# Rank-20 last products from the third token tile on, and plain ones for the second

## The chip, the cores and the metric

The kernel runs on one core of one Trainium2 chip. The metric is device time in microseconds of one execution: median 750.37 over three runs of the kernel before (750.37, 750.37, 753.23). The engines are named as in the profile: PE is the matrix engine (PEld its weight loads), DVE is VectorE, ACT is ScalarE, POOL is GpSimd, SP is the engine that issues most transfers.

## The reference

```python
def _attn_ref(q, k, v):                       # (8, 8, 576, 64) each
    scores = scale * np.matmul(q, k.transpose(0, 1, 3, 2))
    ...
    Dmat = np.where(rel >= 0, gamma[:, None, None] ** rel[None, :, :], 0.0)
    return np.matmul(scores * Dmat[None, :, :, :], v)

def _moe_ref(x, w1, w2, w3, w_out):           # x: (4608, 512), w: (512, 768), w_out: (768, 512)
    h = np.maximum(np.maximum(x @ w1, x @ w2), x @ w3)
    return (h @ w_out).astype(np.float32)
```

A retention block (attention with a decay instead of a softmax) makes x, 4608 tokens of 512 values. A feed-forward block takes the maximum of three products with x, called h (768 values a token), and multiplies it by w_out. All matrices are fp32 (the four weights come as fp64 words and are converted on the chip).

## The kernel before

The 4608 tokens are cut into 9 tiles t = 0 to 8 of 512 tokens. A tile has three stages of work, interleaved on PE: the attention of the next tile, in small matmuls; the three products with w1, w2, w3, called up; and the last product with w_out, called downs. Tile 0 runs while the weights are still converted, and takes its products plainly (`up_plain`, `downs_plain`).

For later tiles `up` (L756 for its matmuls) forms the three products by a scheme with 20 products in place of 24, in five chains A to E; it writes h in three groups fp of 256 hidden values, in the order 0, 2, 1. A product is two matmuls of 128x256. ACT copies chain values to tiles called `part` (L741), and DVE joins them by additions and maxima into h (L744).

`downs` takes the last product by a scheme of seven products in place of eight. Tokens, outputs and hidden values are each split in two; `sums_of_hidden` (L517) forms four sums of h for each group (two on DVE, two on POOL), and `sums_of_outs` forms, once, in tile 1, sums of w_out called To. Each of the seven products has six matmuls of 128x256, two for each group, that add up in one PSUM bank: dx, dy, dz, with two pools of banks, `ps_x` and `ps_y`, of two banks each. The order is written out by hand: 1 in dx, 2 in dy, 6 in dx, 7 in dz, 5 in dx, 4 in dz, 3 in dx. After a product ACT copies its bank to a `part` (`kept`, L560, or L605 for an output), or DVE adds a `part` to it (`total`, L570) and SP stores the result, 256 KB at a time. In the last tile dx is three pieces in banks of their own, so that the last copy and store are small.

Other work is put between the matmuls by hand. `soon` appends steps of VectorE and loads to a queue `urgent`; `chore(n)` emits n of them, or of a second queue, `chores`; `scale(n)` emits n of ACT's scalings of v by head (L191). Each `yield` of `ffn` lets the main loop emit the next entry of `steps(t)`: loads, transposes, scores (L310), values (the o matmuls, L427 and L434) of the next tile. In `downs` the yields stand after the products 2 and 4, and `values` of the next tile's last chunks come at the first of them.

Waits between engines are put in by the framework, from the tiles that instructions read and write; each engine then runs its queue in order.

Of the kernel before, what the change touches and what calls it, by code (L numbers as in the profile page):

```python
# [48 lines left out]
C = 128  # L49
# [25 lines left out]
         "A7": [("A1", ("A1", "B6"), ALU.add), ("A1", ("A1", "A5"), ALU.max), ("A1", ("A1", "A7"), ALU.max)]}  # L75
X_SUMS, W_SUMS = ([x.split() for x in text.split(",")] for text in (X_SUMS, W_SUMS))
PRODUCTS = [x.split() for x in PRODUCTS.split(",")]
# [4 lines left out]
def kernel(  # L82
# [33 lines left out]
    opool = ctx.enter_context(tc.tile_pool(name="opool", bufs=2))  # L116
# [32 lines left out]
    low = const.tile([P, P], FP32, name="low")  # L149
    for c in range(2):  # L150
        r = slice(D * c, D * (c + 1))
        nc.gpsimd.tensor_copy(low[r, 0:D], causal[r, r])
# [150 lines left out]
    def chunk_scores(g):  # L303
# [12 lines left out]
        def mask():  # L316
            nc.vector.tensor_tensor(st[:], s[:], low[:, 0:D].unsqueeze(1).to_broadcast([P, H, D]), op=ALU.mult)
# [137 lines left out]
    def sums_of_x(t, i):  # L455
        if i == CPT - 1 and t > 0:
            xS[t] = {f"a{r + 1}{d + 1}": xT[t][:, d, NH * r:NH * (r + 1)] for r in range(2) for d in range(NDC)}
            xS[t].update(late["X"])
            made[t] = {n for n in xS[t] if n[0] == "a"}

            def step(n, dst, _, a, sign, b):
                combine(*(xS[t][x] for x in (dst, a, b)), sign)
                if dst not in (later[0] for later in X_SUMS[n + 1:]):
                    made[t].add(dst)

            for n, line in enumerate(X_SUMS):
                soon(partial(step, n, *line))
# [36 lines left out]
    def sums_of_outs():  # L504

        pool = late["pool"]
        lo, hi = slice(0, DM // 2), slice(DM // 2, DM)
        b11, b12, b21, b22 = (w_out[:, :, e, r] for e in range(2) for r in (lo, hi))
        t1, t2, t4 = (pool.tile([P, NF // 2, DM // 2], FP32, name=f"To{n}")[:] for n in (1, 2, 4))

        sums = ((t1, b12, b11), (t2, b22, t1)), ((b12, b22, b12), (t4, b21, t2))
        late["sums of T"] = [partial(nc.vector.tensor_tensor, *(x[:, fp] for x in step), op=ALU.subtract)
                             for steps in sums for step in steps for fp in (0, 2, 1)]
        late["T"] = {1: b11, 2: b21, 3: b22, 4: t4, 5: t1, 6: t2, 7: b12}
        late["S"] = {n: pool.tile([P, NF // 2, NH], FP32, name=f"H{n}") for n in (1, 2, 3, 4)}

    def sums_of_hidden(h, fp):  # L517
        s1, s2, s3, s4 = (late["S"][n][:, fp, :] for n in (1, 2, 3, 4))
        a11, a12, a21, a22 = (h[:, 2 * fp + e, NH * r:NH * (r + 1)] for r in range(2) for e in range(2))
        vec, pool = nc.vector.tensor_tensor, nc.gpsimd.tensor_tensor  # L520
        urgent.append(lambda: vec(s1, a21, a22, op=ALU.add))
        urgent.append(lambda: vec(s2, s1, a11, op=ALU.subtract))
        urgent.append(lambda: (pool(s3, a11, a21, op=ALU.subtract), pool(s4, a12, s2, op=ALU.subtract)))  # L523

    def downs(t, h, order):

        def raw_hidden(r, e):
            return lambda fp: h[:, 2 * fp + e, NH * r:NH * (r + 1)]

        def summed(n):  # L530
            return lambda fp: late["S"][n][:, fp, :]

        NM = NH // P
        whole = slice(None)
        last = t == N // NT - 1
        hS = {1: raw_hidden(0, 0), 2: raw_hidden(0, 1), 3: summed(4), 4: raw_hidden(1, 1),
              5: summed(1), 6: summed(2), 7: summed(3)}

        banks = {}

        def bank(pool, tag, name):
            b = pool.tile([P, NM, DM // 2], FP32, tag=tag, name=name)
            pieces = [(m, whole, b[:, m, :]) for m in range(NM)]
            banks[id(pieces)] = [(whole, whole, b[:])]
            return pieces

        def together(src):
            return banks.get(id(src), src)

        def product(n, out, first):  # L550
            for fp in order:
                for m, cols, o in out:
                    nc.tensor.matmul(o, lhsT=hS[n](fp)[:, m * P:(m + 1) * P], rhs=late["T"][n][:, fp, cols],  # L553
                                     start=first and fp == order[0] and (m == 0 or last and out is x),
                                     stop=fp == order[-1], skip_group_check=True)

        def kept(src):
            both = ppool.tile([P, NM, NH], FP32, tag="part", name="part")
            for m, cols, o in together(src):
                nc.scalar.copy(both[:, m, cols], o)  # L560
            return both

        def store(r, c, osb, blocks=slice(None), cols=whole, queue=nc.sync):
            block = out[t * NT + r * NH:t * NT + (r + 1) * NH, c * (DM // 2):(c + 1) * (DM // 2)]
            queue.dma_start(block.rearrange("(m p) d -> p m d", p=P)[:, blocks, cols], osb[:, blocks, cols])

        def total(r, c, src, others):
            osb = opool.tile([P, NM, DM // 2], FP32, tag="osb", name="osb")
            for m, cols, o in together(src):
                nc.vector.tensor_tensor(osb[:, m, cols], o, others[:, m, cols], op=ALU.add)  # L570
            store(r, c, osb)

        if last:
            pieces_of_x = [(0, whole, ps_x), (1, slice(0, DM // 4), ps_r), (1, slice(DM // 4, DM // 2), ps_r)]
            x = []
            for m, cols, pool in pieces_of_x:
                b = pool.tile([P, NH], FP32, tag="x" if pool is ps_x else "r", name="dx")
                x.append((m, cols, b[:, :len(range(NH)[cols])]))
        else:
            x = bank(ps_x, "x", "dx")  # L580
        product(1, x, True)
        p1 = kept(x)
        yield
        y = bank(ps_y, "y", "dy")
        product(2, y, True)
        total(0, 0, y, p1)
        yield
        product(6, x, False)
        u2 = kept(x)
        yield  # L590
        z = bank(ps_y, "y", "dz")
        product(7, z, True)
        p7 = kept(z)
        yield
        product(5, x, False)
        total(1, 1, x, p7)
        yield
        product(4, z, False)
        total(1, 0, z, u2)
        yield  # L600
        osb = opool.tile([P, NM, DM // 2], FP32, tag="osb", name="osb")
        for group in ([[piece] for piece in x] if last else [x]):
            product(3, group, False)
            for m, cols, o in together(group):
                nc.scalar.copy(osb[:, m, cols], o)  # L605
            queue = nc.scalar if last and group[0] is x[-1] else nc.sync
            store(0, 1, osb, slice(group[0][0], group[-1][0] + 1), group[0][1], queue)
        yield
# [109 lines left out]
    def late_room():  # L718
        pool = late["pool"]
        late["W"] = [pool.tile([P, NF, P], FP32, name=f"n{n}") for n in range(1, 9)]  # L720
        late["X"] = {n: pool.tile([P, NH], FP32, name=n)[:] for n in sorted({x[0] for x in X_SUMS})}
# [40 lines left out]
    def downs_plain(t, h):  # L762

        ps = [(ps_x, ps_y)[m % 2].tile([P, DM], FP32, tag="xy"[m % 2], name="down") for m in range(NT // P)]
        for fb in range(NF):
            for m, b in enumerate(ps):
                nc.tensor.matmul(b[:], lhsT=h[:, fb, m * P:(m + 1) * P], rhs=w_sb["out", fb],  # L767
                                 start=(fb == 0), stop=(fb == NF - 1))
                if fb == NF - 1:
                    osb = opool.tile([P, DM], FP32, tag="osb", name="osb")  # L770
                    nc.scalar.copy(osb[:], b[:])
                    nc.sync.dma_start(out[t * NT + m * P:t * NT + (m + 1) * P, :], osb[:])
# [39 lines left out]
    def ffn(t):  # L812

        h = hpool.tile([P, NF, NT], FP32, tag="h", name="h")
        if t == 0:
# [19 lines left out]
            for fb, _ in enumerate(downs_plain(t, h)):  # L835
                convert(2 if fb < 2 else 4 * len(pieces))
                if fb == 2:
                    while_converting.close()
                    late["pool"] = ctx.enter_context(tc.tile_pool(name="late", bufs=1))
                    state_factors()  # L840
                    late_room()
                    sums_of_outs()
# [8 lines left out]
        if t == 1:  # L851
            spread.append(True)
            weight_sums(2)
            weight_sums(1)
        total = len(order) * 2 * len(PRODUCTS)
        count = parts = 0
        for fp in order:
# [13 lines left out]
            sums_of_hidden(h, fp)  # L871
        chore(len(urgent))
        for n, _ in enumerate(downs(t, h, order)):
            if t == 1 and n in (0, 2):
                for step in late["sums of T"][3 * n:3 * n + 6]:
                    step()  # L876
            chore(4)
            scale(2)
            if n in (1, 3):
                yield  # L880
# [148 lines left out]
```

## Time and profile before

| | |
|---|---|
| runs | 750.37, 750.37, 753.23 us |
| profiled execution | 749.71 us, of which the span is 748.0 |
| granted clock of PE | 1.00 |
| busy, of the span | PE 99%, PEld 82%, DVE 69%, ACT 44%, POOL 9% |
| one tile's window (338 to 417 us) | PE 79.0 of 79 us, DVE 52.1, ACT 35.1, POOL 7.8 |

In the groups of the profile a row has the line, the engine, the operation, output and inputs, the shape, the count, then total busy time and the mean of one in ns, and the idle time of the engine just before them with its releaser. In the timeline a row has the start, the length, the engine, the line, the operation and the count; a group of a matmul's records is merged to one row, and the ends of matmuls are modelled. In the chain of waits a row has start, length, engine, tile and count.

### The profile page before, as it was taken

To read this page: it belongs to the slowest core of one execution; us is meant where nothing else is said; L and a number is where in the kernel's file an instruction comes from. 1 tells how busy PE (TensorE), PEld (TensorE's weight loads), DVE (VectorE), ACT (ScalarE), POOL (GpSimd) and SP (SyncE) were. 2 spreads that over 40 slices of the span, in tenths; PEclk is the share of its full clock that TensorE was granted. 3 is DMA by queue.
4 is the path that set the end of the run, shared out by engine and by line. 5 is a ranking of instruction groups with operands and counts; after the bars stand their busy time and mean duration, and the time that the engine had idled before them with its cause. 6 is when DMAs were issued, how large, how long until landed. Compare 5 with 4: busy or idle time off the path is not lost.

```text
span 748.0 us, 16662 instructions
## 1 busy us (share of the span) xinstructions
PE 742.1 (99%) x6768; PEld 615.2 (82%) x6768; DVE 518.5 (69%) x884; ACT 327.1 (44%) x657; POOL 69.3 (9%) x85
## 2 busy tenths in 40 slices
PE   8999999999999999999999999999999999999998
PEld 7645547888888888888888888888888888888887
DVE  3998989998766765686667756774767656763662
ACT  4664533454245424543354435543554255414441
POOL 3000000022000100010010101010101010100000
PEclk9999999999999999999999999999999999999999
DMA  9996742515242514241434224232514141000001
GB/s 224 237 254 140 210 92 74 97 18 96 64 81 46 99 38 95 42 84 44 96 62 73 57 67 90 47 78 61 100 27 88 55 88 31 2 29 29 1 0 57
DMA packets 230205, 59.31 MB, mean 79 GB/s; under 512 B 210800, under 2 KB 228848, under 8 KB 230128
## 3 DMA queue, kind: packets, MB, share of 16 engines
q1 hardware_dynamic: 228720, 57.91, 35.5%
q8 instruction: 53, 0.87, 0.5%
q10 hardware_dynamic: 1408, 0.33, 0.2%
q14 instruction: 24, 0.20, 0.1%
HBM read 48.76 MB, written 9.44 MB: 78 GB/s over the span
## 4 chain that ended last, share of the span: by engine, by line
PE 97%; DVE 1%; DMA 1%; issue 0%; ACT 0%; POOL 0%; POOLq 0%; DVEq 0%
PE a L756 19%; PE b L756 17%; PE dx L553 11%; PE c L756 9%; PE up L780 8%; PE d L756 6%; PE dz L553 6%; PE e L756 6%; PE sk L310 3%; PE down L767 3%; PE dy L553 2%; PE o L427 2%; PE o L434 2%; PE s L288 1%; DMA qraw<-in_q_dram 1%; PE o L396 1%
## 5 line engine op out<-in xcount | busy, mean ns | idle before, releaser
L744 DVE TENSOR_TENSOR part<-part 128x512 f32<-128x512 f32 x168 | 116.0, 691 | 104.8 <-ACT part L741 102.3
L741 ACT COPY part<-b 128x512 f32<-128x512 f32 x120 | 70.2, 585 | 150.6 <-PE b L756 150.5
L744 DVE TENSOR_TENSOR h<-h,part 128x512 f32<-128x512 f32 x120 | 83.7, 697 | 28.1 <-ACT h L741 24.0
L741 ACT COPY part<-a 128x512 f32<-128x512 f32 x96 | 56.2, 585 | 49.9 <-PE a L756 49.2
L756 PE MATMUL a<-s,w 128*128 128x256 f32 x288 | 73.9, 379 | 0.0
L756 PE MATMUL b<-s,n 128*128 128x256 f32 x288 | 73.9, 379 | 0.0
L191 ACT ACTIVATE vraw<-vraw,gk 128x64 f32<-128x64 f32 x208 | 65.4, 346 | 2.2 <-DMA vraw<-in_v_dram 2.1
L780 PE MATMUL up<-xT,w 128*128 128x512 f32 (+2 forms) x160 | 64.0, 554 | 0.0
L756 PEld LDWEIGHTS b<-s,n 128*128 128x128 f32 x288 | 54.7, 190 | 7.4
L756 PEld LDWEIGHTS a<-s,w 128*128 128x128 f32 x288 | 54.7, 190 | 7.4
L780 PEld LDWEIGHTS up<-xT,w 128*128 128x128 f32 x160 | 28.6, 190 | 29.9 <-issue 26.5
L327 POOL TENSOR_TENSOR s<-s,gs_of 64x512 f32<-64x512 f32 x21 | 22.3, 1062 | 320.6 <-DVE s L325 191.2
L756 PE MATMUL c<-xT,w 128*128 128x256 f32 x192 | 51.3, 389 | 0.0
L756 PE MATMUL d<-s,w 128*128 128x256 f32 x192 | 49.8, 380 | 0.0
L756 PE MATMUL b<-xT,n 128*128 128x256 f32 x192 | 49.3, 379 | 0.0
L523 POOL TENSOR_TENSOR H<-h 128x256 f32<-128x256 f32 x24 | 20.2, 843 | 305.3 <-DVE h L744 305.3
L553 PE MATMUL dx<-To,H 128*128 128x256 f32 (+1 forms) x204 | 44.8, 370 | 0.5 <-DVE To L876 0.5
L756 PE MATMUL e<-xT,w 128*128 128x256 f32 x192 | 45.4, 379 | 0.0
L756 PE MATMUL a<-xT,n 128*128 128x256 f32 x192 | 45.4, 379 | 0.0
L553 PEld LDWEIGHTS dx<-To,H 128*128 128x128 f32 x204 | 36.6, 190 | 5.4 <-issue 0.6
L756 PEld LDWEIGHTS e<-xT,w 128*128 128x128 f32 x192 | 36.5, 190 | 5.4 <-issue 0.5
L756 PEld LDWEIGHTS b<-xT,n 128*128 128x128 f32 x192 | 36.5, 190 | 5.0
(123 smaller groups left out, 1288.2 us busy)
## 6 DMA issues: line engine op xcount, KB each, us to landing
bits<-in_moe_w_dram SPq DMA_DIRECT2D x36, 256.0 KB, 5.3
out_dram<-osb SPq DMA_DIRECT2D x35, 256.0 KB, 2.2
kraw<-in_k_dram SPq DMA_DIRECT2D x32, 256.0 KB, 3.1
vraw<-in_v_dram SPq DMA_DIRECT2D x32, 256.0 KB, 3.7
qraw<-in_q_dram SPq DMA_DIRECT2D x224, 32.0 KB, 2.2
kxraw<-in_k_dram SPq DMA_DIRECT2D x224, 32.0 KB, 2.1
bits<-in_moe_w_out_dram SPq DMA_DIRECT2D x6, 512.0 KB, 7.5
qraw<-in_q_dram SPq DMA_DIRECT2D x6, 256.0 KB, 5.5
```

The costliest lines, as they stand in the source:

```text
L191: scaling.popleft()()
L310: nc.tensor.matmul(s[half(c), h, :], lhsT=kT[half(c), h, :], rhs=qT[half(c), h, :], start=True, stop=True)
L327: nc.gpsimd.tensor_tensor(new, new, factor, op=ALU.mult)
L427: nc.tensor.matmul(o[m][half(c), n, u, :], lhsT=vds[g][half(m), h, :], rhs=sts[g][half(m), h, :], start=n == 0 and u == 0, stop=place(g, m ...
L434: nc.tensor.matmul(o[m][half(c), n, u, :], lhsT=stacks[g][half(m), h, :], rhs=qks[g]["q"][half(m), h, :], start=False, stop=True, skip_gro ...
L523: urgent.append(lambda: (pool(s3, a11, a21, op=ALU.subtract), pool(s4, a12, s2, op=ALU.subtract)))
L553: nc.tensor.matmul(o, lhsT=hS[n](fp)[:, m * P:(m + 1) * P], rhs=late["T"][n][:, fp, cols], start=first and fp == order[0] and (m == 0 or l ...
L741: nc.scalar.copy(of[step], ps[step[0]][:])
L744: nc.vector.tensor_tensor(of[dst], a, b, op=op)
L756: nc.tensor.matmul(ps[chain][:, e, :], lhsT=factor(w, 2 * fp + e), rhs=xS[t][x], start=n == 1 and e == 0, stop=ends, skip_group_check=True)
L767: nc.tensor.matmul(b[:], lhsT=h[:, fb, m * P:(m + 1) * P], rhs=w_sb["out", fb], start=(fb == 0), stop=(fb == NF - 1))
L780: nc.tensor.matmul(ps[:, a:b], lhsT=w_sb[i, fb][:, dc * P:(dc + 1) * P], rhs=xT[t][:, dc, a:b], start=dc == 0 and a == 0, stop=dc == NDC - ...
```

## The change

From tile 2 on, `downs` takes the last product by a scheme of 20 products in place of 24: three groups of hidden values by four blocks of 128 tokens by two halves of outputs. The products are listed in `DOWNS` as chain, factor of h, factor of w_out, and run in nine chains C to I that lie in halves of four banks: E and G in one, I and H in one, F and C in one, D in one. `TOTALS` lists what follows after which product: a copy by ACT (`k1 = I`, L567 in the changed kernel) or a sum by DVE; results y are stored 128 KB at a time. The factors of h are formed by 19 sums on DVE (`HIDDEN_SUMS`): those of the first two groups are queued as chores while `up` goes on, those of the last group stand at the head of `downs`. The factors of w_out are formed once, in tile 2, by 11 sums (`OUT_SUMS`). The yields stand after the products 4 and 10.

Tile 1 takes its last product plainly, in 24 matmuls of 128x512, in the order of the groups. The sums To and H and POOL's part in them go. To make room, a mask called low is folded into another, one sum of x is formed in place, and the buffers of results are four of half the size.

```diff
+DOWNS = """I b13 c13, H n1 m14, H n5 v15, E b12 c12, F n7 c22, G n8 c22, E b11 c11, I n2 m6, H b41 v19, I b43 m7,
+           H b42 c12, I n4 m11, G n3 c21, I b33 c23, D n6 c21, I b32 v10, C b22 v13, I b23 v3, C b31 c11, I b21 v22"""
+
+TOTALS = {1: "k1 = I", 2: "k14 = H", 3: "k15 = H", 7: "y11 = E + k1", 8: "k6 = I", 9: "k19 = H", 10: "k7 = I",
+          11: "y14 = H - k6, k19 = k19 - k6", 12: "k11 = I, k14 = k11 - k14, y24 = F + k14", 13: "y21 = G - k11",
+          14: "k20 = I", 15: "y23 = D + k20", 16: "k10 = I, k1 = k1 + k10", 17: "u = C + k7, u = u + k19",
+          18: "k3 = I, y12 = u - k3", 19: "k7 = C + k7, y13 = k7 - k1", 20: "y22 = I - k15"}
...
-    opool = ctx.enter_context(tc.tile_pool(name="opool", bufs=2))
+    opool = ctx.enter_context(tc.tile_pool(name="opool", bufs=4))
...
     def downs(t, h, order):
+        n8, n23, n6 = (ppool.tile([P, m, 2, P], FP32, tag="part", name="n") for m in (1, 2, 1))
+        late_ones = {"n8": n8[:, 0], "n2": n23[:, 0], "n3": n23[:, 1], "n6": n6[:, 0]}
+        for step in sums_of_hidden(h, order, 1, late_ones):
+            step()
         banks = {}
+        for pool, tag, chains in ((ps_y, "y", "EG"), (ps_y, "y", "IH"), (ps_x, "x", "D"), (ps_x, "x", "FC")):
+            b = pool.tile([P, 2, DM // 2], FP32, tag=tag, name="d" + chains.lower())
+            banks.update({chain: b[:, n] for n, chain in enumerate(chains)})
...
+        for n, (chain, b, v) in enumerate(DOWNS):
+            begins = chain in "IEFD" and chain not in begun
+            begun.add(chain)
+            for e in range(2):
+                nc.tensor.matmul(banks[chain], lhsT=hidden(h, order, b, late_ones)[:, e], rhs=late["V"][v][:, e],
+                                 start=begins and e == 0, stop=chain not in [x[0] for x in DOWNS[n + 1:]] and e == 1,
+                                 skip_group_check=True)
+            for line in TOTALS.get(n + 1, ()):
+                total(*line)
+            yield
...
+        if t == 2:
+            out_sums(order)
...
+            if t > 1 and fp != order[-1]:
+                chores.extend(sums_of_hidden(h, order, 3 - order.index(fp)))
+        chore(len(urgent) + len(chores))
+        if t == 1:
+            for n, _ in enumerate(downs_plain(t, h, order)):
+                chore(5)
+                scale(3)
+                if n in (1, 3):
+                    yield
+        else:
+            for n, _ in enumerate(downs(t, h, order)):
+                chore(2)
+                scale()
+                if n in (3, 9):
+                    yield
         yield
```

More of the change, by code (lines that the diff above doesn't have):

```diff
@@ L75 @@
          "A7": [("A1", ("A1", "B6"), ALU.add), ("A1", ("A1", "A5"), ALU.max), ("A1", ("A1", "A7"), ALU.max)]}
+HIDDEN_SUMS = {3: "b33 = b13 + b33, n1 = b13 + b43",
+               2: "n4 = b33 - b32, b43 = b43 + n4, b23 = b43 - b23, n7 = b42 + n4, n5 = b22 + b23, b23 = b32 + b23,"
+                  "b42 = b42 - n5",
+               1: "n8 = b12 - n4, n2 = n1 - b41, b43 = b41 - b43, b41 = b41 - n5, n3 = b11 - n2, b21 = b21 - b41,"
+                  "b22 = b22 - b21, n6 = b31 + n2, b32 = b22 - b32, b31 = b31 + b32"}
+OUT_SUMS = """m14 = -c21 - c23, m6 = m14 - c13, v19 = c11 - m6, v15 = c12 + v19, v22 = c22 + v15, v3 = v15 + m14,
+              m7 = -c13 - c23, m11 = m7 - c22, v13 = c12 - m11, v10 = c11 + v13, c23 = c22 + c23"""
+DOWNS = """I b13 c13, H n1 m14, H n5 v15, E b12 c12, F n7 c22, G n8 c22, E b11 c11, I n2 m6, H b41 v19, I b43 m7,
+           H b42 c12, I n4 m11, G n3 c21, I b33 c23, D n6 c21, I b32 v10, C b22 v13, I b23 v3, C b31 c11, I b21 v22"""
+TOTALS = {1: "k1 = I", 2: "k14 = H", 3: "k15 = H", 7: "y11 = E + k1", 8: "k6 = I", 9: "k19 = H", 10: "k7 = I",
[3 rows of a table added]
 X_SUMS, W_SUMS = ([x.split() for x in text.split(",")] for text in (X_SUMS, W_SUMS))
-PRODUCTS = [x.split() for x in PRODUCTS.split(",")]
+PRODUCTS, DOWNS, OUT_SUMS = ([x.split() for x in text.split(",")] for text in (PRODUCTS, DOWNS, OUT_SUMS))
+HIDDEN_SUMS, TOTALS = ({n: [x.split() for x in text.split(",")] for n, text in table.items()}
+                       for table in (HIDDEN_SUMS, TOTALS))
 WAHEAD = 6
@@ L148 @@
                             base=0, channel_multiplier=-1, pattern=[[1, C]])
[L149 to L152, printed above, removed]
     def warm(n):
@@ L316, in mask @@
         def mask():
-            nc.vector.tensor_tensor(st[:], s[:], low[:, 0:D].unsqueeze(1).to_broadcast([P, H, D]), op=ALU.mult)
+            nc.vector.tensor_tensor(st[:], s[:], causal[:, 0:D].unsqueeze(1).to_broadcast([P, H, D]), op=ALU.mult)
         def keep_chunk(c):
@@ L458, in sums_of_x @@
             xS[t].update(late["X"])
+            xS[t]["s13"] = xS[t]["a12"]
             made[t] = {n for n in xS[t] if n[0] == "a"}
@@ L502, in load_weights @@
                     nc.sync.dma_start(blocks[half(c)], heads[:, head(c, 0):head(c, NP)])
[L504 to L523, printed above, removed]
@@ L525, in downs @@
-    def downs(t, h, order):
[L527 to L537, printed above, removed]
-        banks = {}
[L541 to L608, printed above, removed]
@@ new lines, in groups, with out_sums, step @@
+    def groups(order):
+        return dict(zip((3, 2, 1), (slice(2 * fp, 2 * fp + 2) for fp in order)))
+    def out_sums(order):
+        forms = late["V"]
+        for i in range(2):
+            for g, fp in zip((3, 2, 1), order):
+                forms[f"c{i + 1}{g}"] = w_out[:, fp, :, i * DM // 2:(i + 1) * DM // 2]
+        def step(dst, _, a, sign, b):
+            if a[0] == "-":
+                nc.vector.scalar_tensor_tensor(out=forms[dst], in0=forms[a[1:]], scalar=-1.0, in1=forms[b],
+                                               op0=ALU.mult, op1=ALU.subtract)
+            else:
+                combine(forms[dst], forms[a], forms[b], sign)
+        chores.extend(partial(step, *line) for line in OUT_SUMS)
@@ new lines, in hidden, with sums_of_hidden, total @@
+    def hidden(h, order, name, late_ones={}):
+        if name[0] == "n":
+            return late_ones[name] if name in late_ones else late["N"][name]
+        j, g = int(name[1]), int(name[2])
+        return h[:, groups(order)[g], P * (j - 1):P * j]
+    def sums_of_hidden(h, order, g, late_ones={}):
+        return [partial(combine, *(hidden(h, order, n, late_ones) for n in (dst, a, b)), sign)
+                for dst, _, a, sign, b in HIDDEN_SUMS[g]]
+    def downs(t, h, order):
+        n8, n23, n6 = (ppool.tile([P, m, 2, P], FP32, tag="part", name="n") for m in (1, 2, 1))
+        late_ones = {"n8": n8[:, 0], "n2": n23[:, 0], "n3": n23[:, 1], "n6": n6[:, 0]}
+        for step in sums_of_hidden(h, order, 1, late_ones):
+            step()
+        banks = {}
+        for pool, tag, chains in ((ps_y, "y", "EG"), (ps_y, "y", "IH"), (ps_x, "x", "D"), (ps_x, "x", "FC")):
+            b = pool.tile([P, 2, DM // 2], FP32, tag=tag, name="d" + chains.lower())
+            banks.update({chain: b[:, n] for n, chain in enumerate(chains)})
+        begun, parts = set(), {}
+        def total(dst, _, a, sign=None, b=None):
+            a, b = (banks.get(x, parts.get(x)) for x in (a, b))
+            if dst[0] == "y":
+                place = opool.tile([P, DM // 2], FP32, tag="osb", name="osb")[:]
+            else:
+                if dst not in parts:
+                    parts[dst] = ppool.tile([P, DM // 2], FP32, tag="part", name=dst)[:]
+                place = parts[dst]
+            if sign is None:
+                nc.scalar.copy(place, a)
+            else:
+                combine(place, a, b, sign)
+            if dst[0] == "y":
+                i, j = int(dst[1]) - 1, int(dst[2]) - 1
+                nc.sync.dma_start(out[t * NT + j * P:t * NT + (j + 1) * P, i * DM // 2:(i + 1) * DM // 2], place)
+        for n, (chain, b, v) in enumerate(DOWNS):
[8 more added lines that the diff above has]
+            yield
@@ L719, in late_room @@
         pool = late["pool"]
+        late["N"] = {n: pool.tile([P, 2, P], FP32, name="h" + n)[:] for n in ("n1", "n4", "n5", "n7")}
+        late["V"] = {n: pool.tile([P, 2, DM // 2], FP32, name=n)[:] for n, *_ in OUT_SUMS if n != "c23"}
         late["W"] = [pool.tile([P, NF, P], FP32, name=f"n{n}") for n in range(1, 9)]
-        late["X"] = {n: pool.tile([P, NH], FP32, name=n)[:] for n in sorted({x[0] for x in X_SUMS})}
+        late["X"] = {n: pool.tile([P, NH], FP32, name=n)[:] for n in sorted({x[0] for x in X_SUMS} - {"s13"})}
     converting = convert_all()
@@ L760, in up, with downs_plain @@
                 yield
-    def downs_plain(t, h):
+    def downs_plain(t, h, order):
+        blocks = [2 * fp + e for fp in order for e in range(2)]
         ps = [(ps_x, ps_y)[m % 2].tile([P, DM], FP32, tag="xy"[m % 2], name="down") for m in range(NT // P)]
-        for fb in range(NF):
+        for fb in blocks:
             for m, b in enumerate(ps):
                 nc.tensor.matmul(b[:], lhsT=h[:, fb, m * P:(m + 1) * P], rhs=w_sb["out", fb],
-                                 start=(fb == 0), stop=(fb == NF - 1))
-                if fb == NF - 1:
-                    osb = opool.tile([P, DM], FP32, tag="osb", name="osb")
+                                 start=fb == blocks[0], stop=fb == blocks[-1])
+                if fb == blocks[-1]:
+                    osb = ppool.tile([P, DM], FP32, tag="part", name="osb")
                     nc.scalar.copy(osb[:], b[:])
@@ L834, in ffn @@
             convert(3)
-            for fb, _ in enumerate(downs_plain(t, h)):
+            for fb, _ in enumerate(downs_plain(t, h, range(NF // 2))):
                 convert(2 if fb < 2 else 4 * len(pieces))
@@ L840, in ffn @@
                     state_factors()
+                    nc.gpsimd.tensor_copy(causal[half(1), 0:D], causal[half(1), half(1)])
                     late_room()
-                    sums_of_outs()
                     weight_sums(0)
@@ L870, in ffn @@
                     yield
[L871 to L880, printed above, removed]
+            if t > 1 and fp != order[-1]:
[7 more added lines that the diff above has]
+                    yield
+        else:
+            for n, _ in enumerate(downs(t, h, order)):
[3 more added lines that the diff above has]
+                    yield
         yield
```

## The prediction

> **What bounds the kernel now.** I read the page first, then the table of PE's waits, then the chain of waits through one tile.
>
> ```profile
> span 748.0 us, 16662 instructions
> ...
> PE 742.1 (99%) x6768; PEld 615.2 (82%) x6768; DVE 518.5 (69%) x884; ACT 327.1 (44%) x657; POOL 69.3 (9%) x85
> ...
> PE 97%; DVE 1%; DMA 1%; issue 0%; ACT 0%; POOL 0%; POOLq 0%; DVEq 0%
> ```
> ```profile
> PE warm L158 <- POOL ident masks.py:199: 1.4, 1, 1.4
> PE qt L274 <- DMA qraw<-in_q_dram: 1.1, 1, 1.1
> PE dx L553 <- DVE To L876: 0.5, 1, 0.5
> ```
>
> PE carries 97% of the chain, and after the start-up it waits once, for 0.5 us, in tile 1. So the time is the sum of PE's records, and a change counts in two ways only: records added or removed, and waits put in PE's queue. The chain (start, length, what) gives a record's price:
>
> ```profile
> 654.74 2.59 PE dx L553 x12
> 657.33 2.59 PE dy L553 x12
> ...
> 676.82 0.86 PE b L756 x4
> ```
>
> An fp32 matmul is two records, so these 12 records are 6 matmuls of 128x256: 2.59/12 = 0.216 us a record, 0.432 a matmul, 0.864 for a product of two.
>
> Now the timeline at the same place:
>
> ```profile
> 654.58 2.75 PE L553 MATMUL dx<-w_out,h 128*128 128x256 f32 x12
> ...
> 656.92 2.21 DVE L744 TENSOR_TENSOR h<-h,part 128x512 f32<-128x512 f32 x3
> ...
> 657.17 2.75 PE L553 MATMUL dy<-w_out,h 128*128 128x256 f32 x12
> 657.37 0.58 ACT L560 COPY part<-dx 128x512 f32<-128x512 f32 x1 [2.00 <-PE dx L553]
> ```
>
> The copy of dx starts 0.04 us after dx's last record ends (654.58 + 2.75 = 657.33) and runs while PE works in another bank, dy. Each copy is covered by a whole product of 2.59 us. That cover is what the change touches.
>
> **Records.** Tiles 2 to 8 had 7 products of 12 records, 84 x 0.216 = 18.14 us; now 20 of 4, 80 x 0.216 = 17.28. That is -0.864 a tile, -6.05 for seven. The last tile also loses its split pieces (2.63 us a dx product instead of 2.59, four times): -0.18. Tile 1 becomes 24 matmuls of 128x512, priced by tile 0's:
>
> ```profile
> 115.70 7.13 PE L767 MATMUL down<-w_out,h 128*128 128x512 f32 x16
> ```
>
> That group holds 0.43 us a record (a longer group of 32 takes 13.90), so 48 x 0.43 = 20.6 instead of 18.14: +2.5. The stall on To goes with the sums of T: -0.6 with its restart. Nothing is late in its place: plain products take the groups in order (0,2,1), so the last group is touched 13.8 us after the start, and its values are ready 4.6 us after it. Tile 1: +1.9.
>
> **Waits.** Of the 20 products, chains I and H lie in the two halves of one bank, as E and G, and F and C. In the built program a matmul into either half waits for the last copy out of that bank, whichever half it read: product 2 (H) waits for k1 (of I), 3 for k14, 9 for k6, 10 for k19, 11 for k7 (all ScalarE copies), 12 for y14 (a VectorE subtraction). In these six the copied product stands directly before the waiting one and PE has nothing in between. The later ones (14 for k11, 16 for k20, 18 for k10, 20 for k3, 19 for u) have one product in between.
>
> No stage of before has such a wait, so I compose it. Copy and total of 128x256 out of PSUM:
>
> ```profile
> L560 ACT COPY part<-dx 128x256 f32<-128x256 f32 x2 | 0.7, 372 | 6.1 <-PE dx L553 6.1
> L570 DVE TENSOR_TENSOR osb<-dx,part 128x256 f32<-128x256 f32 x1 | 0.4, 425 | 6.4 <-issue 6.4
> ```
>
> How PE restarts after a wait:
>
> ```profile
> 47.62 1.23 DVE L652 TENSOR_TENSOR w<-mant,expo 128x1024 f32<-128x1024 f32 x1
> 47.79 0.19 PEld L780 LDWEIGHTS up<-xT,w 128*128 128x128 f32 x1 [0.24 <-issue]
> 48.22 0.19 PEld L780 LDWEIGHTS up<-xT,w 128*128 128x128 f32 x1 [0.24 <-issue]
> 48.90 0.37 PEld L780 LDWEIGHTS up<-xT,w 128*128 128x128 f32 x2 [0.49 <-DVE w L652]
> 49.51 0.19 PEld L780 LDWEIGHTS up<-xT,w 128*128 128x128 f32 x1 [0.24 <-issue]
> ```
> ```profile
> 6.35 0.58 ACT L275 COPY qT<-qt 128x512 f32<-128x512 f32 x1 [0.47 <-PE qt L274]
> ...
> 7.10 0.97 PEld L288 LDWEIGHTS s<-qT,kT 64*128 64x128 f32 x16 [0.23 <-ACT qT L275]
> ```
>
> VectorE ended at 48.85, the load began at 48.90 and was not hidden: loads start with the record before theirs, so 49.51 is the second record and, 0.43 earlier, 49.08 the first. Restart 0.23 after the release. After ScalarE (6.93) the load began 0.17 later.
>
> One wait: from the start of the copied product's last record 0.38 (its length) + 0.04 + 0.372 + 0.23 = 1.02 us until the next product flows, instead of 0.216. Lost: 0.81; for y14, with 0.425, 0.86. A tile: 5 x 0.81 + 0.86 = 4.91; seven tiles +34.4. From below: the weight load hides and only 0.05 remains of the restart: 0.63 a wait, +26.8. From above: 0.17 and a whole load of 0.19: 0.94 a wait, +39.8. I take the middle, since a full load was exposed in the one row that shows PE's main shape. With one product in between, the next flows 0.216 + 0.864 = 1.08 after that record anyway, and 1.02 is inside it: nothing, and at the upper bound 0.07 x 4 x 7 = +2.0.
>
> One page speaks against the change as a whole. The Trainium skill, "PSUM — Partial Sum Buffer", section "PSUM bank collisions raise a hardware error", asks for waits by bank and quadrant, not by address. Guarded by address only product 3 would wait, and by these rows the sum would be about 751; guarded by bank it is the one below. The trace of before shows only copies whose bank PE has left.
>
> **VectorE, ScalarE, stores.** VectorE gains 19 sums of h and 14 totals and loses 6 sums and 3 totals of double width a tile: 52.1 us of 79 plus 33 x 0.42 less 2.9 less 2.1 is 61, of 83. It matters only where PE waits for it. Counting from the first product: the joins of the last group end at 4.6 us (656.92 + 2.21 - 654.58); ten late sums at 0.33 to 0.45 apart, 8.5; two xT, 9.8; ten sums of x and y11, 13.7. The 11th product ends at 11 x 0.864 + 2.1 (the o matmuls of attention) + 5 x 0.81 = 15.7, so y14 starts at once: cover 2 us, and beyond it every microsecond is paid, with the later totals, transposes and stores queued behind. n8, late by 5.0, is needed by product 6 at 8.0. The attention block moves from behind product 2 to behind product 4, from 5.2 to 5.1 us: nothing. ScalarE fits copy and scaling (0.372 + 0.346) into a product that now lasts 1.67. The two early groups' sums and tile 2's 11 sums of w_out (0.69 each) lie in the up stage, where VectorE idles a third: nothing, or up to 2 us if they delay joins. Six POOL operations a tile go, off the path. Eight stores of 128 KB replace four; each waits in SP's queue for a total, with loads for later chunks behind it that are used a stage later. Tail: a total of 0.425 instead of a copy of 0.27 before the last store: +0.2.
>
> **Sum.** 749.7 (748.0 span plus 1.7 around it) - 6.05 - 0.18 + 1.9 + 34.4 + 0.2 = 780.0. The profiled execution lies 0.7 under the median 750.37. With the bounds 772.4 and 787.4 (with the 2.0).
>
> **Rivals.**
> - *The waits cost nearly nothing* (not slower). If a copy releases PE inside the product's own flow, the sum without waits is 745.6. The place is product 2, 3, 9 to 12; break-even is 4.8/42 = 0.11 us a wait. At 0.05 it gives 747.7. Against it: 0.372 of copying alone is over three times that, and PE has one queue. It could also be that the totals are ordered otherwise on the chip than built, but each engine runs its queue in order. 3%.
> - *Part of it is hidden*, the last record's end being modelled: 0.4 a wait, 762. 6%.
> - *VectorE comes late.* Two transposes (0.69 each) standing ahead of y14 or u add up to 1.4 a tile: 790. For: they are in the same queue at this place. Against: in the order built they follow y14, and 2 us of cover. 7%.
> - *The clock drops.* From product 8 to 12 PE would be busy about half of the time. At half the clock that stretch, 5 x 0.864, would cost 4.3 more a tile: 810. Against: at 4 to 28 us, with gaps of 1 us, the granted clock is 1.00, as everywhere. The Trainium skill's "TensorE: Matmul & The Clock Gate", section "A second HAM failure mode: psum-queue depth-cycling", tells of a clock that falls in such a pattern; no row here shows it. 4%.
> - The forecast, 772 to 788 with its bounds: 80%.
>
> **Chances and range.** 0.5% (3.8 us) is about what a measurement of this kernel can tell from no change. Faster holds the first rival's greater part, 2%; same 2%; slower 96%. The range, 770 to 791, is the bounds, 2 us below for rounding and half of VectorE's case above.
>
> **What would show it.** PE's waits should list ScalarE copies of the new downs some 35 times and VectorE some 7 times, at 0.5 to 0.8 us each; PE idle should go from 6 to over 30 us; the stretch from the first product of a tile's downs to the next tile's e should go from 20.3 to some 24.4 us; the clock should stay at 1.00. It would be wrong if the records follow each other through products 8 to 12 without gaps, or if a gap sits before products 14 to 20.

## The result, and the profile after

The changed kernel takes 785.58 us (median of five runs, 785.01 to 786.27) against 750.77 for the kernel before (five runs, 750.37 to 753.23): a ratio of 1.046, 95% interval 1.0441 to 1.0478. It is slower, by 35 us. The profiled execution is the run of 786.03 us, of which the span is 784.0.

The head of the page:

```profile
span 784.0 us, 16725 instructions
...
PE 750.7 (96%) x6680; PEld 599.1 (76%) x6680; DVE 571.4 (73%) x1040; ACT 336.5 (43%) x693; POOL 28.2 (4%) x36
...
PEclk9999999999999999999999999999999999999999
```

PE has 88 records fewer (6680 for 6768), yet its span grew by 36 us. Its idle time went from 748.0 - 742.1 = 5.9 us to 784.0 - 750.7 = 33.3. The granted clock is full in all 40 slices. VectorE is busier (571.4 for 518.5), POOL hardly works any more.

The table of PE's waits (waiting engine, tile and line, releaser, then us in total, times, longest):

```profile
PE dih L578 <- ACT k L567: 16.8, 35, 0.5
PE sk L323 <- DVE qT L209: 4.9, 6, 1.1
PE dih L578 <- DVE osb L484: 4.1, 7, 0.6
PE warm L171 <- POOL ident masks.py:199: 1.4, 1, 1.4
```

The first and the third row are the six waits a tile that were forecast: 35 on a ScalarE copy, 7 on a VectorE subtraction, all on the bank dih, that of I and H (the chains C to I are seven in four banks, not nine). The second row was not forecast: once a tile the scores of the next tile (sk) wait for the transposed queries (qT).

PE's timeline through the last product of tile 2 (start, length, engine, line, what; in brackets the idle time before it and its releaser):

```profile
264.51 1.03 PE L578 MATMUL dih<-w_out,h 128*128 128x256 f32 x4
266.00 1.13 PE L578 MATMUL dih<-m,hn 128*128 128x256 f32 x4 [0.46 <-ACT k L567]
267.59 1.13 PE L578 MATMUL dih<-v,hn 128*128 128x256 f32 x4 [0.46 <-ACT k L567]
...
274.23 1.03 PE L578 MATMUL dih<-m,n 128*128 128x256 f32 x4
275.76 1.13 PE L578 MATMUL dih<-v,h 128*128 128x256 f32 x4 [0.51 <-ACT k L567]
277.40 1.13 PE L578 MATMUL dih<-m,h 128*128 128x256 f32 x4 [0.51 <-ACT k L567]
279.00 1.13 PE L578 MATMUL dih<-w_out,h 128*128 128x256 f32 x4 [0.46 <-ACT k L567]
280.71 1.13 PE L578 MATMUL dih<-m,hn 128*128 128x256 f32 x4 [0.59 <-DVE osb L484]
281.68 1.03 PE L578 MATMUL deg<-w_out,n 128*128 128x256 f32 x4
282.54 1.03 PE L578 MATMUL dih<-w_out,h 128*128 128x256 f32 x4
```

Each row is one product. In flow one starts 0.86 us after the other (281.68 to 282.54). Up to a waiting one the step is 1.49 (264.51 to 266.00), 1.59, 1.53, 1.64, 1.60 and 1.71, and from a waiting one to the next that flows it is 0.97 (280.71 to 281.68). The bracket shows only 0.46 to 0.59 of that: the rest is counted as busy, since a product that stands alone lasts 1.13 in the trace, and in flow it takes 0.86. So the price of a wait is not its number in the table of waits. I take it from whole stretches, measured on PE's timeline from the first product of each stage to the first of the next:

| stretch, us | before | after |
|---|---|---|
| start to the first downs of tile 0 | 98.48 | 99.49 |
| downs of tile 1 | 20.93 | 22.82 |
| downs of tiles 2 to 7, each | 20.35 | 24.07 to 24.08 |
| up of tile 1 | 58.46 | 58.46 |
| up of tiles 2 to 7 | 58.46 each | 59.54, 59.89, 59.56, 59.56, 59.53, 59.52 |
| up of tile 8 (no next tile) | 51.80 | 51.81 |
| downs of tile 8 and tail | 21.26 | 25.20 |

The 36.0 us by which the span grew are found in it: start +1.0, tile 1 +1.9, the downs of six tiles 6 x 3.73 = +22.4, six ups +6.8, the last tile +3.9.

### The profile page after: what moved, and what is told of

It is laid out like the page before. It is cut to its first block, busy times and chain, and to the rows that moved or that the text cites. A ratio compares the mean times of both kernels' runs of the same rounds, so it can differ in the third digit from the quotient of the medians.

```text
span 784.0 us, 16725 instructions
## 1 busy us (share of the span) xinstructions
PE 750.7 (96%) x6680; PEld 599.1 (76%) x6680; DVE 571.4 (73%) x1040; ACT 336.5 (43%) x693; POOL 28.2 (4%) x36
## 5 line engine op out<-in xcount | busy, mean ns | idle before, releaser
L721 DVE TENSOR_TENSOR part<-part 128x512 f32<-128x512 f32 x168 | 117.1, 697 | 97.9 <-ACT part L718 95.4
L721 DVE TENSOR_TENSOR h<-h,part 128x512 f32<-128x512 f32 x120 | 83.6, 697 | 24.0 <-ACT h L718 19.7
L567 ACT COPY k<-dih 128x256 f32<-128x256 f32 x70 | 26.1, 372 | 112.0 <-PE dih L578 77.9
L204 ACT ACTIVATE vraw<-vraw,gk 128x64 f32<-128x64 f32 x208 | 67.6, 348 | 4.6 <-DMA vraw<-in_v_dram 4.6
L733 PE MATMUL a<-xT,w 128*128 128x256 f32 x192 | 49.3, 379 | 0.0
L733 PE MATMUL a<-s,w 128*128 128x256 f32 x192 | 49.3, 379 | 0.0
L340 POOL TENSOR_TENSOR s<-s,gs_of 64x512 f32<-64x512 f32 x21 | 22.4, 1066 | 558.1 <-DVE s L338 508.6
L745 PE MATMUL down<-w_out,h 128*128 128x512 f32 x96 | 42.1, 594 | 0.0
L733 PEld LDWEIGHTS a<-xT,w 128*128 128x128 f32 x192 | 36.5, 190 | 5.0
L733 PEld LDWEIGHTS a<-s,w 128*128 128x128 f32 x192 | 36.5, 190 | 5.0
```

Of the source, the lines that this page charges most:

```text
L204: scaling.popleft()()
L340: nc.gpsimd.tensor_tensor(new, new, factor, op=ALU.mult)
L567: nc.scalar.copy(place, a)
L721: nc.vector.tensor_tensor(of[dst], a, b, op=op)
L733: nc.tensor.matmul(ps[chain][:, e, :], lhsT=factor(w, 2 * fp + e), rhs=xS[t][x], start=n == 1 and e == 0, stop=ends, skip_group_check=True)
```

## The experiments

My theory: the six waits, which come from I and H lying in one bank, are worth over 4 us a tile, and the sums of h that stand among the transposes 1.1. The rivals of each run stand in its expectation. All edits are against the changed kernel, and where a run builds on an earlier one only what comes on top is shown; a time is a median, and the ratio is to the kernel before, measured on the same chip.

### I and H in two banks

```diff
-        for pool, tag, chains in ((ps_y, "y", "EG"), (ps_y, "y", "IH"), (ps_x, "x", "D"), (ps_x, "x", "FC")):
+        for pool, tag, chains in ((ps_y, "y", "EG"), (ps_y, "y", "I"), (ps_x, "x", "HD"), (ps_x, "x", "FC")):
...
-            begins = chain in "IEFD" and chain not in begun
+            begins = chain in "IEFH" and chain not in begun
```

> Chain H moves from I's bank to D's; nothing else. If the lost time of the downs is PE waiting for the last copy out of a shared bank, five of the six waits in a row go (products 2, 9, 10, 11, 12; 0.73 + 0.77 + 0.77 + 0.73 + 0.85 = 3.85 us a tile by the changed kernel's timeline), product 3 keeps its own: 785.6 - 7 x 3.85 = 758.6. Rival one, VectorE's queue takes the wait's place: with PE earlier, u would come about 1.9 us after PE wants product 19, so about 772. Rival two, waits go by address and the gaps are ScalarE being late: no change, 785.

Measured: 758.05 us (757.96 to 759.21), 1.0102 (1.008 to 1.0124). PE's waits:

```profile
PE sk L323 <- DVE qT L209: 4.9, 6, 1.1
PE dhd L578 <- ACT k L567: 3.2, 7, 0.5
```

Only the wait between products 2 and 3, both into H, is left, once a tile. The downs fell from 24.07 to 20.27 us, 3.80 for five waits: 0.76 each. The copies, the totals and the products are the same ones, so the shared bank was what PE waited for. The sk row and the ups are unchanged, and no wait for u has taken the place of the five (the first rival).

The Trainium skill, "PSUM — Partial Sum Buffer", section "PSUM bank collisions raise a hardware error", says that a different address in the same bank and quadrant is no protection, and asks for guards by bank and quadrant. The waits of the built program are laid out like that, and this run puts their price at 0.76 us each; what a kernel without them would do was not tried.

### Product 4 before product 3

```diff
-DOWNS = """I b13 c13, H n1 m14, H n5 v15, E b12 c12, F n7 c22, ...
+DOWNS = """I b13 c13, H n1 m14, E b12 c12, H n5 v15, F n7 c22, ...
-TOTALS = {1: "k1 = I", 2: "k14 = H", 3: "k15 = H", ...
+TOTALS = {1: "k1 = I", 2: "k14 = H", 4: "k15 = H", ...
```

> The products 3 and 4 change places (H n5 after E b12), so that the copy k14 has a product to hide behind; the banks stay. By the bank theory one wait of six goes: 785.6 - 7 x 0.73 = 780.5. If only a copy of the same half made PE wait, this was the one such place, and all of the 4.58 us a tile would go: 753.5.

Measured: 779.67 us (779.48 to 780.53), 1.039 (1.0364 to 1.0416).

```profile
PE dih L578 <- ACT k L567: 13.6, 28, 0.5
```

28 waits for 35, and the downs 23.35 us for 24.08: 0.73 for the one wait that is gone. One product in between covers the copy, without a change of banks.

### Sums of h only when no transpose or load is queued

```diff
-                elif chores:
+                elif chores and (t == 1 or not urgent):
```

> From tile 2 on a sum of h is emitted only when no step is urgent, so that none comes between the transposes of the next tile's chunks and the scores that wait for them. If these sums delay the transposes, the up stages of tiles 2 to 7 fall from 59.5 to 58.5 us each: 785.6 - 6.8 = 778.8. If VectorE is late as a whole, from the downs before, the up stages stay: 785.

Measured: 778.32 us (777.97 to 778.56), 1.0368 (1.0347 to 1.039). In the table of PE's waits both rows on dih are as they were (16.8 and 4.1 us), and the sk row is gone. The ups are 58.46 to 58.49 us again. What had happened is in VectorE's timeline, first of the changed kernel, in the up of a middle tile:

```profile
416.51 0.71 DVE L209 STREAM_TRANSPOSE kT<-kxraw 128x512 f32<-128x512 f32 x1
417.15 0.38 DVE L484 TENSOR_TENSOR h<-h,hn 128x256 f32<-128x256 f32 x1
417.57 0.42 DVE L484 TENSOR_TENSOR h<-h 128x256 f32<-128x256 f32 x1
417.91 0.42 DVE L484 TENSOR_TENSOR hn<-h,hn 128x256 f32<-128x256 f32 x1
418.25 0.68 DVE L721 TENSOR_TENSOR part<-e,part 128x512 f32<-128x512 f32 x1
418.85 0.70 DVE L209 STREAM_TRANSPOSE qT<-qraw 128x512 f32<-128x512 f32 x1
```

The same place in this experiment:

```profile
412.40 0.70 DVE L209 STREAM_TRANSPOSE kT<-kxraw 128x512 f32<-128x512 f32 x1
413.03 0.65 DVE L721 TENSOR_TENSOR part<-e,part 128x512 f32<-128x512 f32 x1
413.60 0.69 DVE L209 STREAM_TRANSPOSE qT<-qraw 128x512 f32<-128x512 f32 x1
414.21 0.38 DVE L484 TENSOR_TENSOR hn<-h 128x256 f32<-128x256 f32 x1
```

Two transposes that PE's scores need lay 2.34 us apart (416.51 to 418.85) with three sums of h and a join (L721) between them, and lie 1.20 apart, with the join alone between them, when the sums come after. These sums have no date until the downs. VectorE was idle enough on the average; it was the order of its queue that made PE wait.

### All three edits together

> The three edits together. If the parts add up: 785.6 - 27.0 - 5.1 - 6.8 = 746.7, below the kernel before. If VectorE's queue becomes the bound of the downs once PE's waits go, 1.9 to 2.5 us a tile come back at product 19: 760 to 764.

Measured: 750.83 us (750.28 to 751.49, ten runs), 1.0004 (0.9993 to 1.0015): level with the kernel before, and 4 us over the sum of the parts. The longest of PE's waits:

```profile
PE dfc L578 <- DVE u L484: 2.6, 5, 0.5
```

With the old waits gone PE is early enough to meet a new one: product 19 goes into the bank of F and C, and waits for u, the total of product 17, in tiles 2 to 6. There the downs are 20.27 us, in tile 7, which has no tile after the next one, 19.49: 5 x 0.78 = 3.9, the missing time. It is the second case of the expectation, at 0.78 us a tile in place of 1.9 to 2.5. VectorE's rows, with the products 17 and 19 of PE, show why:

```profile
277.68 0.71 DVE L209 STREAM_TRANSPOSE kT<-kxraw 128x512 f32<-128x512 f32 x1
277.93 1.03 PE L578 MATMUL dfc<-v,h 128*128 128x256 f32 x4
278.30 0.39 DVE L484 TENSOR_TENSOR osb<-deg,k 128x256 f32<-128x256 f32 x1
278.61 0.69 DVE L209 STREAM_TRANSPOSE qT<-qraw 128x512 f32<-128x512 f32 x1
279.23 0.38 DVE L484 TENSOR_TENSOR osb<-dhd,k 128x256 f32<-128x256 f32 x1
279.54 0.40 DVE L484 TENSOR_TENSOR k<-k,k 128x256 f32<-128x256 f32 x1
279.86 0.41 DVE L484 TENSOR_TENSOR u<-dfc,k 128x256 f32<-128x256 f32 x1
280.33 1.13 PE L578 MATMUL dfc<-w_out,h 128*128 128x256 f32 x4 [0.51 <-DVE u L484]
```

Product 17 starts at 277.93 and its records end at 278.96, but u starts at 279.86: two transposes for a later tile stand in the queue ahead of it, among three totals, without a gap between any of VectorE's rows. So a second theory: product 19 waits because the steps of later tiles that `chore(2)` emits after each product delay u.

### Three places for those steps

Three kernels with all three edits, and one thing more each. First, no steps after the 11th product; what is left of them goes to the up stage:

```diff
-                chore(2)
+                chore(2 if n < 11 else 0)
```

> As the three edits together, but from the 12th product on no step of the next tile is emitted between the totals, so that u is not queued behind sums of x and transposes. If VectorE's queue is what holds product 19 (0.78 us in each of tiles 2 to 6), the downs fall from 20.27 to 19.49 and the time to 750.8 - 5 x 0.78 = 746.9. Rival: the steps put off make the up stage late instead, as they did in the changed kernel (1.1 us a tile): 750 to 752.

Measured: 758.78 us (757.58 to 758.97), 1.0113 (1.0097 to 1.0129). The downs of tiles 2 to 7 fell to 19.49 us, which bears the second theory out, but the ups of tiles 3 to 7 rose to 60.39 to 61.29:

```profile
PE sk L323 <- DVE qT L209: 8.1, 5, 1.6
```

The rival of that expectation held, and cost more than it said: the steps that were put off come in front of the next transposes, and the scores wait 1.6 us, five times.

Second, the steps stay, and the totals that read no bank (u's second sum, y12, y13, k19, k1) go to POOL:

```diff
...
-                combine(place, a, b, sign)
+                combine(place, a, b, sign, nc.gpsimd if dst in ("u", "y12", "y13", "k19", "k1") and not in_bank else nc.vector)
```

> As the three edits together, but five totals that read no PSUM (k19, k1, the second step of u, y12, y13) go to POOL. Two of them stand before u, so VectorE reaches it some 0.8 us sooner: 746.9 if that is enough. Rival: POOL and VectorE slow each other (before, the sums beside POOL's took 0.554 us instead of 0.418) and the gain is lost: 750 to 751.

Measured: 750.96 us (749.78 to 755.68), 1.002 (1.0005 to 1.0035). The listed wait for u halved (1.3 us for 2.6), but the downs went only from 20.27 to 20.14, and in tile 7 and the last tile they grew (19.49 to 19.73, 21.35 to 21.71): a POOL sum takes 0.72 us in this run, VectorE's 0.42. There is no gain; the transposes still stand ahead of u, which starts 0.65 us after the end of its product in place of 0.90.

Third, the steps that were put off are emitted behind u, four after each of the last products:

```diff
-                chore(2)
+                chore(2 if n < 11 else 0 if n < 16 else 4)
```

> As the three edits together, but between the 12th and the 17th product no step of the next tile is emitted, and the ones left over come right behind u (four a product), ahead of the up stage. If it was the place in VectorE's queue that mattered both for u and for the transposes, the downs of tiles 2 to 6 fall from 20.27 to 19.49 and the ups stay at 58.5: 750.8 - 5 x 0.78 = 746.9. Rival: the totals k7 and y22 now come late for the banks that the next up stage takes: 1 to 2 us a tile at its fourth product, 751 to 758.

Measured: 748.04 us (746.19 to 750.51, twelve runs), 0.9975 (0.9965 to 0.9985). The downs are 19.49 us and the ups 58.46 to 58.49, both at PE's own rate. The products 17 and 19 and u in the same tile:

```profile
277.81 1.03 PE L578 MATMUL dfc<-v,h 128*128 128x256 f32 x4
278.87 0.42 DVE L484 TENSOR_TENSOR u<-dfc,k 128x256 f32<-128x256 f32 x1
279.53 1.03 PE L578 MATMUL dfc<-w_out,h 128*128 128x256 f32 x4
```

Now u starts 0.03 us after its product ends, and product 19 does not wait; the second theory holds. Past the start PE waits once, in the last tile, where product 6 waits for n8 (0.5 us).

### Rank 20 in tile 1 as well

The first of these three, with tile 1 by rank 20 too; the 11 sums of w_out stand at the head of tile 1, nine of them on POOL.

```diff
-        if t == 2:
+        if t == 1:
             out_sums(order)
...
-        if t == 1:
+        if t < 1:
             for n, _ in enumerate(downs_plain(t, h, order)):
...
```

> As e5_defer, and tile 1 too takes the scheme of 20 products; the sums of w_out are made at the head of tile 1, nine on POOL and two on VectorE. By PE's records tile 1's downs fall from 22.82 to 19.5, so 746.9 - 3.3 = 743.6. Rival: VectorE, busy 63.5 of 68 us in tile 1 before, cannot take 19 sums and 14 totals more there, and the wait shows in tile 1's up stage: 747 to 752.

Measured: 768.23 us (766.3 to 769.48), 1.0242 (1.0222 to 1.0261). The downs of tile 1 fell to 19.48 us as expected, its up rose from 58.46 to 68.75 (and that of tile 2 to 60.38, as in the later tiles of the first of the three). The largest piece of the 10.3 us in PE's waits:

```profile
PE d L734 <- DVE part L722: 5.7, 1, 5.7
```

VectorE was late, and its timeline at the start of tile 1, beside POOL's, shows one reason:

```profile
138.98 1.33 POOL L533 TENSOR_TENSOR v<-w_out,v 128x512 f32<-128x512 f32 x1
139.10 1.49 DVE L484 TENSOR_TENSOR n<-w,n 128x256 f32<-128x256 f32 x1
140.27 1.44 POOL L533 TENSOR_TENSOR w_out<-w_out 128x512 f32<-128x512 f32 x1
140.51 1.48 DVE L484 TENSOR_TENSOR n<-w,w 128x256 f32<-128x256 f32 x1
141.92 0.41 DVE L484 TENSOR_TENSOR w<-w,w 128x256 f32<-128x256 f32 x1
```

A VectorE sum of 128x256 takes 0.41 us once POOL is done (the last row), and 1.48 or 1.49 as long as POOL's sums run; eight such rows, and one of 0.89, lie between 129 and 142 us. At some 1.07 each that is about 9 us of VectorE's time. A join with one input in a bank (L722, 0.68 us) is not stretched. That POOL stretched them is read from the moment at which the rows change, not from a run of its own. The Trainium skill, "SBUF — State Buffer", section "SBUF: two separate sides", tells of a pair of ports that a VectorE operation with two SBUF inputs and a GpSimd operation that reads SBUF hold by turns, a whole instruction at a time; the rows agree: the sum that starts at 139.10 ends at 140.59, 0.28 us after POOL's sum of 138.98 to 140.31.

The stretch is not all of the 10.3 us. VectorE also has nine sums of h more in this up (3.8 us), where it was busy 51.5 of 58.5 us without them (the first of the three; the 63.5 of 68 us in the expectation fit only a window that takes in the end of tile 0); no run tells the two apart. And the wait was followed by a slow stretch of PE:

```profile
163.53 1.22 PE L734 MATMUL d<-s,w 128*128 128x256 f32 x2 [5.68 <-DVE part L722]
169.32 1.09 PE L734 MATMUL b<-xT,n 128*128 128x256 f32 x4
```
```profile
PEclk9999999989999999999999999999999999999999
```

From the product d that waited to the next b 5.79 us went by, and 3.09 at the same place in the first of the three. The granted clock was 0.50 from 162.6 to 169.5 us: about 2.7 us of the 10.3 are the clock's.

### The best version: n8 formed a group earlier

The third of the three, and n8 = b12 - n4 is formed in the second group instead of at the head of the downs, in a tile of its own, for which one of the four result buffers goes.

```diff
-               2: "n4 = b33 - b32, b43 = b43 + n4, ...
-               1: "n8 = b12 - n4, n2 = n1 - b41, ...
+               2: "n4 = b33 - b32, n8 = b12 - n4, b43 = b43 + n4, ...
+               1: "n2 = n1 - b41, ...
...
```

> As e8_after_u, and the sum n8 is made with those of the second group instead of behind the last joins (three result buffers instead of four make room for it). In the last tile, which has no attention between the products, product 6 waits 0.46 us and a restart for n8; that goes: 0.7 less than e8_after_u, 746.2. Rival: three result buffers make a total wait for a store: some tenths a tile more, 747 to 749.

Measured: 746.25 us (745.41 to 746.94, five runs), 0.9946 (0.9933 to 0.9959): faster than the changed kernel, and 4 us (0.5%) under the kernel before, with an interval clear of 1. The page and PE's two longest waits:

```profile
PE 737.5 (99%) x6680; PEld 601.6 (81%) x6680; DVE 573.7 (77%) x1040; ACT 336.5 (45%) x693; POOL 28.5 (4%) x36
```
```profile
PE warm L171 <- POOL ident masks.py:199: 1.4, 1, 1.4
PE up L758 <- DVE w L627: 1.2, 1, 1.2
```

Both belong to the start. The last stretch is 20.62 us, for 21.35 with the wait for n8: 0.7 of the 1.8 us between the two medians, and the runs of the kernel before this one spread over 4.3. The downs of tiles 2 to 7 stay at 19.49, so no total that waits for a store shows. The records are the 6680 of the changed kernel, and PE's busy time is 13.2 us less than there. That is what waits add to a "busy" PE: the downs of the changed kernel lost 7 x 4.58 = 32.1 us and the table of waits lists 20.9 of it, the ups lost 6.8 and it lists 4.9; 13.1 are left.

| waits in one product after the other, a tile | downs, us | kernel |
|---|---|---|
| 6 | 24.08 | changed |
| 5 | 23.35 | product 4 before 3 |
| 1 | 20.27 | I and H in two banks |
| 0 | 19.49 | steps behind u |

## Why the prediction was right, and where its sum was off

The forecast was 780.0 us and slower; the time is 785.58, inside the range, and the mechanism is the one forecast: records saved, more time lost in six waits. Two errors partly cancel, 2.3 us too much for the waits and 6.8 too little for the ups. By its steps:

- **Records.** -0.864 a tile was said. Without waits the downs are 19.49 for 20.35 of before: -0.86. Tile 1 was to get 1.9 longer and got 22.82 - 20.93 = 1.89. The sum without any wait, 745.6, is nearly what the best version reaches, 746.25.
- **Waits.** Places, counts (35 and 7) and releasers are those named. The size was a little high: 4.91 a tile was said, 24.07 - 19.49 = 4.58 measured, 0.76 each and not 0.81, inside the bounds 0.63 to 0.94. The term that was too large is the restart of PE, 0.23, taken from a row with a whole weight load exposed. In all engines' timeline after the first copy:

```profile
265.57 0.37 ACT L567 COPY k<-dih 128x256 f32<-128x256 f32 x1 [0.28 <-PE dih L578]
...
265.99 0.73 PEld L578 LDWEIGHTS dih<-m,hn 128*128 128x128 f32 x4 [0.86 <-ACT k L567]
266.00 1.13 PE L578 MATMUL dih<-m,hn 128*128 128x256 f32 x4 [0.46 <-ACT k L567]
```

  The copy ends at 265.94, the load starts 0.05 later, and the product's records take 0.10 more than in flow (1.13 for 1.03): 0.15 in place of 0.23. With it the price of a wait is 0.73, the lower end of what the steps between two waiting products show (1.59 to 1.64, less 0.86); for y14 0.86 was said, and 1.71 - 0.86 = 0.85 is measured.
- **The later products.** Products 14 to 20, with one product in between, lose nothing (281.68, 282.54 and on): right. So is the cover of y14: it starts as soon as its product ends. But the same cover for u was there only because PE was late. When PE's waits were taken away, u came 0.9 us late, and 0.78 a tile went to it. That is the rival on VectorE, with its mechanism as written (two transposes ahead of u), at about half its price and only in a kernel that the forecast was not about.
- **Sums in the up stage.** This is the step that was mis-sized: "nothing, or up to 2 us if they delay joins", and nothing in the sum. It was 6.8 us, 1.06 to 1.43 in each of six ups, and what the sums delayed were transposes, not joins. The argument was that VectorE idles a third of the time there. What counted was the place of the sums in its queue, between two transposes that PE's scores wait for; I had not followed who waits for what stands behind the added sums. That the time still falls into the range is in part luck: its upper end was made for dearer waits and for a late VectorE in the downs, neither of which came, and the ups took up that room.
- **The rest.** The start of this execution was 1.0 us longer than that of before; in eight of the experiments' traces, with no edit to it, it lies between 97.83 and 99.57 (in that with rank 20 in tile 1 it is 101.11), so I count it as scatter. The last tile gained 3.9 where 4.1 follows from the sum. Together: 780.0 + 6.8 for the ups + 1.0 for the start - 7 x 0.33 for the waits + 0.3 for what lies around the span (2.0, not 1.7) = 785.8, and 786.03 was profiled. In the range, the upper bound 787.4 and half of VectorE's case (4.9) make 792, not 791; nothing hangs on it.
- **The rivals.** Waits at nothing, or at half, are out (0.73 to 0.78 each, on the mean, in three kernels). The clock stayed at 1.00, also between 270 and 280 us, where PE was busy 8.5 of 10 us, and between 274 and 282, where it was busy 5.9 of 8.

## What to carry to other kernels

When a scheme with fewer products is cut into more and smaller ones, look up for every product which one stands before it in the same bank: one other product in between hid a copy here, with none the wait cost twice the copy's 0.37 us. An added operation on an engine with idle time is priced by what stands behind it in that queue, not by the idle share. And after each wait that is taken away, ask what was on time only because of it: here the third layer of waits (product 19 on u) took back 4 us of the gain, and they came back only when the steps ahead of u were put right behind it; left for the next stage, they made the scores wait.

## What was unexpected of the hardware

- PE restarts cheaply after a wait: 0.05 us from the end of ScalarE's copy to the weight load, 0.10 more in the product.
- The table of waits shows 0.46 to 0.59 us for waits that cost 0.76 on the mean; the rest, 11 us in all, is booked as busy time.
- VectorE's sums of two SBUF tiles took 1.49 us instead of 0.41 while POOL was adding.
- The granted clock stayed at 1.00 through six waits of 0.76 us within 20 products, and through PE's five gaps of 1.6 us in the kernel that emits no steps after the 11th product. With rank 20 in tile 1 it fell to 0.50 when PE had stood still for 4.8 us of its wait of 5.7, and stayed there for 6.8 us; in the same trace it was 0.50 for 3.4 us in the start too, after a gap of 1.7. So these runs give no threshold.
